# One down-projection chunk, loaded partly apart: 512 columns over seven transfer engines where it was 320 columns over four

## The chip, the cores and the metric

The kernel runs on one core of one Trainium2 chip. The metric is device time in microseconds (us) of one execution. The kernel before takes 265.25 us, the median of 3 runs (265.12 to 265.45).

## The reference, cut to what matters

One decode step of a block with attention and a gated MLP, 8 sequences, model width 1024, all in 32-bit floats:

```python
h  = x + attention(layernorm(x), wq, k_cache[-1024:], v_cache[-1024:], wo)
g  = layernorm(h) @ w_gate          # 1024 x 3584
u  = layernorm(h) @ w_up            # 1024 x 3584
h2 = h + (gelu(g) * u) @ w_down     # 3584 x 1024
```

Only the last product is touched by the change. Its 3584 rows are 28 chunks of 128 rows (q = 0 to 27); chunk 19 is the one that the change is about. There are only 8 rows of activations, so nearly all the work is to bring in the weights and caches.

## The kernel before, in words

**Stages.** The weights and caches pass once through one large buffer in on-chip memory (`space`, 2 x 16384 columns of 128 partitions), in the order wq, k, v, wo, gate and up (`gu`), down (`dn`), each with large transfers of 128 partitions, all issued by SyncE (SP) through the helper `move` (L89 to L92; its DMA start is on L91). A transfer is issued as soon as the part of the buffer that it overwrites has been used. Matmuls (4 copies of the 8 activation rows make 32 columns of weights for TensorE, PE) run when a transfer has landed; a wait for a transfer is a wait until all 16 transfer engines have finished their part of it.

**Transfers and engines.** A transfer's rows (one a partition) are dealt evenly over the transfer engines: 128 rows over all 16, 8 rows each; 4 rows over four engines, one row each, which the words of the change call the first four. Each engine works through its own queue in the order of issue, so an engine that got more bytes, or was held up, is late in all that follows.

**Down.** `PARTS = (8, 8, 4, 4, 2, 1)` (L27) cuts chunks 0 to 26 into six transfers, wd0 to wd5; here they are called the first to the sixth `dn` transfer. Chunk 27 comes in two transfers of its own (`ends`). The issue loop is L424 to L443, that of the ends L446 to L449. Chunk 19 is the last one of the third transfer (chunks 16 to 19). The last 320 columns (`SIDE_COLS`) of chunk 19 are not in that transfer, which so has 8 x 15104 B per engine in place of 8 x 16384 B; they come just ahead of it in 8 small transfers into `w_side` (L434 to L437): each has 4 partitions, 4 apart, hence the first four engines get one row of 5120 B (4 shares of 320 columns) from each of them, 40960 B in all. Row p of a small transfer's partitions holds 4 rows of the chunk, at different places ("shares").

**What the side rows need.** Chunk 19's activations stand transposed in `at` for the whole chunk. For `w_side` they must stand by partition as the shares do: four more transposes of shifted windows of `hm` (L396 to L399, windows of 48 columns from `SIDE_ROWS`) write them into PSUM behind the chunk transposes, ScalarE (ACT) copies them into `at_side` (L406). VectorE (DVE) copies the ordinary ones to `at` (L400).

**Down matmuls** (L457 to L474): in pairs of chunks, four matmuls of 512 columns a pair into four row groups of one bank `ya`. For chunk 19's second half there is one of 192 columns (L462) and four of 320 columns from `w_side` over 48 partitions (L472). Then `ya` is copied to `d1` by DVE (L476), chunk 26 goes to two other banks (L485), `d1` is added there by matmuls with `add2` (L485 too), chunk 27 follows (L497), ACT copies the two banks out (L500), and two transfers of 64 KB write the result.

Of the kernel before, what the change touches and what calls it, by code (L numbers as in the profile page):

```python
# [7 lines left out]
P = 128  # L8
B = 8
D = 1024  # L10
# [8 lines left out]
N = 512  # L19
# [6 lines left out]

PARTS = (8, 8, 4, 4, 2, 1)  # L27
SIDE = 19
SIDE_COLS = 320
SIDE_ROWS = (0, 16, 64, 80)  # L30
ENDS = (128, 128)
TAIL = 2

# [4 lines left out]
class Flow:  # L38
# [42 lines left out]
    def run(self, engine, make, *waits, mark=True):  # L81
        ins = self.start(engine, make, waits)
        if not mark:
            return None
        self.done[engine] += 1
        ins.then_inc(self.own[engine], 1)
        return self.own[engine], self.done[engine]
# [7 lines left out]
def decode_block(nc, x, wq, kt, v, wo, gu, dn, side, ends, outs):  # L95
# [8 lines left out]
    fl = Flow(nc)  # L104
    run, move = fl.run, fl.move
# [4 lines left out]
    def sb(name, *shape):  # L110
        return nc.alloc_sbuf_tensor(name, list(shape), F32).ap()
# [25 lines left out]
    ta, tb, ya = bank("ta", N), bank("tb", N), bank("ya", N)  # L137
# [10 lines left out]
    ident = sb("ident", P, P)  # L148
# [6 lines left out]
    qz = [sb(f"qz{hf}", P, 2, 10 * 32) for hf in range(2)]  # L155

    h_sb = sb("h_sb", P, D)

    w_side = sb("w_side", 64, len(SIDE_ROWS), SIDE_COLS)
    zero = [run("gpsimd", lambda e, t=t: e.memset(t, 0.0)) for t in (*qz, h_sb, w_side)]  # L160

    spread = sb("spread", P, CP, B)
    run("gpsimd", lambda e: e.tensor_copy(
# [14 lines left out]
    own = sb("own", P, HB)  # L178
# [4 lines left out]
    def transposes(pt, src, n, ready, clear, rows=P):  # L183

        t = pt[:, 0:n * rows].rearrange("p (n r) -> p n r", n=n)
        tok = None
        for i in range(n):
            tok = run("tensor", lambda e, i=i: e.transpose(  # L188
                t[:, i, :], src[:, i * P:(i + 1) * P], ident[:rows, :rows]),
                id_ok, ready, clear, mark=(i == n - 1))  # L190
        return t, tok
# [36 lines left out]
    for hf in range(2):  # L228
        w, w_in, wb = wq_t[hf]
        q_ps = (acc, tb)[hf]  # L230
        for c in range(NC):
            for j in range(NQ):
                tok = run("tensor", lambda e, c=c, j=j: e.matmul(  # L233
                    q_ps[32 * j:32 * j + 32, :], xt[c], w[:, c, j * N:(j + 1) * N],
                    start=(c == 0), stop=(c == NC - 1)),
                    w_in, x_ok, mark=(c == NC - 1 and j == NQ - 1))
        free[wb] = tok
        q_sb = sb(f"q{hf}", P, N)
        tok = run("vector", lambda e: e.tensor_scalar(q_sb, q_ps, scale, None, op0=ALU.mult), tok)
        acc_free = tok  # L240
        qt, tok = transposes(ta, q_sb, N // P, tok, ta_free)
# [54 lines left out]
    for hf in range(2):  # L296
        p_sb, p_ok, share, sh_ok = ps[hf]
        pt = sb(f"pt{hf}", P, KC, P)
        p0, tok0 = transposes(ta, p_sb[:, 0:W // 2], KC // 2, p_ok, ta_free)
# [5 lines left out]
        for c in range(KC):  # L305
            for r in range(NQ):
                s, half = divmod(r, 2)
                tok = run("tensor", lambda e: e.matmul(  # L308
                    o3[32 * r:32 * r + 32], pt[:, c, 32 * r:32 * r + 32],
                    v_t[:, s, c, half * HB:(half + 1) * HB, :],  # L310
                    start=(c == 0), stop=(c == KC - 1)),
                    v_in, ta_free, ya_free, mark=(c == KC - 1 and r == NQ - 1))
# [50 lines left out]
    for k, nb in enumerate(SETS):  # L363
        pair = big[1 - k].rearrange("p (s n) -> p s n", s=2)
        clear = (ps[1][1], h_ok)[k]
        for s in range(2):
            if k == 0:
                w, w_in, wb = load(gu[k][s], f"gu{k}_{s}", "c n", c=NC)
            else:
                n = NC * nb * N  # L370
                w = space[:, place:place + n].rearrange("p (c n) -> p c n", c=NC)
                w_in = move(f"gu{k}_{s}", w, gu[k][s], (used[0, 0], half_used)[s])
                place += n
            for c in range(NC):
                for j in range(nb):
                    tok = run("tensor", lambda e: e.matmul(  # L376
                        pair[32 * j:32 * j + 32, s, :], ht[c], w[:, c, j * N:(j + 1) * N],
                        start=(c == 0), stop=(c == NC - 1)),
                        w_in, ht_ok, clear, mark=(c in (NC // 2 - 1, NC - 1) and j == nb - 1))
                if (k, s, c) == (0, 1, NC // 2 - 1):  # L380
                    half_used = tok
            used[k, s] = tok
            if s == 0:
                rows = 32 * nb
                ge = sb(f"ge{k}", P, N)
                g_ok = run("scalar", lambda e: e.activation(
                    ge[:rows], pair[:rows, 0, :], AF.Gelu_apprx_tanh), tok)
        hm = sb(f"hm{k}", P, N)
        tok = run("vector", lambda e: e.tensor_mul(hm[:rows], ge[:rows], pair[:rows, 1, :]), tok, g_ok)  # L389
        hp, tok = transposes(ta, hm[:rows], N // P, tok, ta_free, rows)  # L390
        if k == 1:

            g, i = divmod(SIDE - q0, N // P)
            sp = ta[0:48, N - 32 * len(SIDE_ROWS):N].rearrange("p (s m) -> p s m", m=32)
            assert g == 0 and rows * (N // P) + 32 * len(SIDE_ROWS) <= N
            for s, c0 in enumerate(SIDE_ROWS):  # L396
                tok = run("tensor", lambda e: e.transpose(
                    sp[:, s, :], hm[0:32, i * P + c0:i * P + c0 + 48], ident[0:32, 0:32]),
                    mark=(s == len(SIDE_ROWS) - 1))  # L399
        ta_free = run("vector", lambda e: e.tensor_copy(  # L400
            at[:, q0:q0 + nb * (N // P), :].rearrange("p (j i) m -> p i j m", j=nb),
            hp.rearrange("p i (j m) -> p i j m", j=nb)), tok)
        at_ok.append(ta_free)
        if k == 1:
            at_side = sb("at_side", 48, len(SIDE_ROWS), 32)
            side_ok = run("scalar", lambda e: e.copy(at_side, sp), ta_free)  # L406
        q0 += nb * (N // P)

# [10 lines left out]
    def rows_of(q):  # L419
        return ring[:, slot(q)]  # L420
# [3 lines left out]
    for i, n in enumerate(PARTS):  # L424


        a, b = slot(q0), slot(q0) + n
        clear = used[0, 1] if a >= base else used[1, 0] if b * D <= place // 2 else used[1, 1]
        assert b <= SLOTS and (a >= base or b <= base)
        if q0 <= SIDE < q0 + n:  # L430
            assert SIDE == q0 + n - 1

            side_in = fl.sem("w_side")
            for h, src in enumerate(side):  # L434
                p0 = h % 4 + 32 * (h // 4)
                fl.start("sync", lambda e: e.dma_start(w_side[p0:p0 + 13:4], src), [zero[-1]]).then_inc(
                    side_in, 16)  # L437
            side_in = side_in, 16 * len(side)
            here = move(f"wd{i}", space[:, a * D:b * D - SIDE_COLS], dn[i], clear)
        else:  # L440
            here = move(f"wd{i}", ring[:, a:b], dn[i], clear)
        arrived.update((q, here) for q in range(q0, q0 + n))
        q0 += n  # L443
    blocks = []
    c0 = 0
# [11 lines left out]
    for q in range(0, first, 2):  # L457
        for i in range(NQ):
            e2, ch = divmod(i, 2)
            r = ch if q in SLOW else i  # L460
            n = N - SIDE_COLS if (q + e2, ch) == (SIDE, 1) else N
            tok = run("tensor", lambda e: e.matmul(  # L462
                ya[32 * r:32 * r + 32, 0:n], at[:, q + e2, :],
                rows_of(q + e2)[:, ch * N:ch * N + n],
                start=(r not in opened), stop=(q == first - 2)),
                arrived[q + e2], at_ok[(q + e2) * P >= SETS[0] * N],
                mark=(q == first - 2 and i == NQ - 1))
            opened.add(r)
            if n < N:
                for s in range(len(SIDE_ROWS)):  # L470
                    r = 1 + 2 * (s % 2)
                    run("tensor", lambda e: e.matmul(  # L472
                        ya[32 * r:32 * r + 32, n:N], at_side[:, s, :], w_side[0:48, s, :],
                        start=False, stop=False), side_in, side_ok, mark=False)  # L474
    d1 = sb("d1", P, N)
    d1_ok = run("vector", lambda e: e.tensor_copy(d1, ya), tok)  # L476

# [125 lines left out]
```

## Time and profile before

| what | value |
|---|---|
| median of 3 runs | 265.25 us |
| span of the profiled execution, first to last instruction | 263.8 us |
| read from memory, and rate over the span | 111.18 MB, 422 GB/s |
| PE busy | 137.9 us (52%) |
| DVE, ACT, POOL busy | 23.3, 10.9, 5.5 us |

The profiled execution has no time of its own beside its span; the median of the runs is 1.45 us above the span. In the rows below, a line of the chain of waits is "start, length, what"; a line of a window table is "window, length, busy time of an engine and number of instructions, granted TensorE clock, share of the 16 transfer engines that was busy, GB/s". Packets are counted in the window in which they start, with their whole length, so a share of a short window can be over 1. A packet of under 512 B stands at the end of an engine's part of each transfer: it is the engine's report that its part is done. So the number of such packets in a window is the number of engines that have finished a transfer in it.

### The profile page before, as it was taken

How to read it: one execution, taken by the hardware profiler on the slowest of the kernel's cores; microseconds unless marked ns; L12 is line 12 of the kernel's file. 1: busy time of each engine (PE TensorE's matmuls, PEld its weight loads, DVE VectorE, ACT ScalarE, POOL GpSimd, SP SyncE). 2: the span in 40 equal slices, each digit the busy share in tenths (PEclk: the TensorE clock that was granted, in tenths of full speed). 3: DMA queues.
4: the chain of work that ended last, by engine and by line, in shares of the span. 5: the costliest groups of instructions: out<-in, count | busy, mean ns of one | idle time of the engine just before them, and what ended most of it. 6: DMA issues, size and time to landing. Idle time of an engine off the chain costs nothing.

```text
span 263.8 us, 2071 instructions
## 1 busy us (share of the span) xinstructions
PE 137.9 (52%) x958; PEld 40.2 (15%) x958; DVE 23.3 (9%) x55; ACT 10.9 (4%) x17; POOL 5.5 (2%) x15
## 2 busy tenths in 40 slices
PE   0015806804905906806707707718509676589875
PEld 0011201201201301301202202112102111123122
DVE  0320100100010020200200100160000200010001
ACT  1110000000010020110000000020000000000000
POOL 8000000000000000000000000000000000000000
PEclk9999975985985895975975956986965979599999
DMA  8998998999799989999998999999899989999995
GB/s 318 482 437 358 477 477 378 420 467 477 328 467 477 420 388 457 470 388 437 447 477 348 460 457 437 398 437 477 360 422 455 477 365 465 412 422 452 390 415 203
DMA packets 3256, 111.44 MB, mean 422 GB/s; under 512 B 392, under 2 KB 648, under 8 KB 1072
## 3 DMA queue, kind: packets, MB, share of 16 engines
q1 hardware_dynamic: 3088, 111.22, 98.0%
q8 instruction: 7, 0.11, 0.2%
q10 hardware_dynamic: 160, 0.10, 0.1%
q14 instruction: 1, 0.01, 0.0%
HBM read 111.18 MB, written 0.13 MB: 422 GB/s over the span
## 4 chain that ended last, share of the span: by engine, by line
DMA 78%; PE 20%; SPq 0%; issue 0%; ACT 0%
DMA w<-gu 20%; DMA w<-wq 16%; DMA w<-kt 12%; DMA w<-wo 11%; DMA w<-v 11%; DMA w<-dn 9%; PE big L376 6%; PE big L261 4%; PE tb L233 4%; PE tb L308 3%; PE ya L336 3%; SPq L91 0%; PE acc L485 0%; ACT o_fin L500 0%; PE tb L485 0%
## 5 line engine op out<-in xcount | busy, mean ns | idle before, releaser
L376 PE MATMUL big<-w,ln_t 128*32 128x512 f32 x224 | 36.1, 730 | 21.6 <-DMA w<-gu 21.6
L261 PE MATMUL big<-w,qz 128*32 128x512 f32 x128 | 18.8, 753 | 20.2 <-DMA w<-kt 20.2
L336 PE MATMUL ya<-w,ot 128*32 128x512 f32 x128 | 18.1, 729 | 19.6 <-DMA w<-wo 19.6
L462 PE MATMUL ya<-w,at 128*32 128x512 f32 (+1 forms) x104 | 16.4, 590 | 3.6 <-DMA w<-dn 3.6
L376 PEld LDWEIGHTS big<-w,ln_t 128*32 128x32 f32 x224 | 9.0, 130 | 47.3 <-issue 25.8
L308 PE MATMUL tb<-w,pt 128*32 128x512 f32 x64 | 9.1, 732 | 9.8 <-DMA w<-v 9.8
L233 PE MATMUL tb<-w,ln_t 128*32 128x512 f32 x64 | 9.2, 743 | 9.2 <-DMA w<-wq 9.2
L308 PE MATMUL acc<-w,pt 128*32 128x512 f32 x64 | 8.5, 694 | 8.6 <-DMA w<-v 8.6
L233 PE MATMUL acc<-w,ln_t 128*32 128x512 f32 x64 | 8.6, 699 | 7.5 <-DMA w<-wq 7.5
L188 PE MATMUL ta<-ident,ln_xn 64*128 64x64 f32 x16 | 2.1, 304 | 19.3 <-DVE ln_xn L214 19.3
L261 PEld LDWEIGHTS big<-w,qz 128*32 128x32 f32 x128 | 4.8, 135 | 33.6 <-issue 23.4
L336 PEld LDWEIGHTS ya<-w,ot 128*32 128x32 f32 x128 | 5.0, 132 | 31.2 <-issue 31.2
L462 PEld LDWEIGHTS ya<-w,at 128*32 128x32 f32 x104 | 4.2, 109 | 15.4 <-issue 10.3
L389 DVE TENSOR_TENSOR hm<-ge,big 128x512 f32<-128x512 f32 (+1 forms) x2 | 1.4, 686 | 56.7 <-PE big L376 56.7
L270 DVE TENSOR_REDUCE nmax<-big 128x1 f32<-128x1024 f32 x2 | 2.5, 1225 | 35.7 <-PE big L261 35.7
L272 ACT ACTIVATE p<-big,nmax 128x1024 f32<-128x1024 f32 x2 | 2.2, 1114 | 78.1 <-DVE nmax L270 78.1
L308 PEld LDWEIGHTS tb<-w,pt 128*32 128x32 f32 x64 | 2.5, 131 | 15.7 <-issue 15.7
L188 PEld LDWEIGHTS ta<-ident,ln_xn 64*128 64x128 f32 x16 | 1.7, 200 | 20.1 <-DVE ln_xn L214 20.1
L233 PEld LDWEIGHTS tb<-w,ln_t 128*32 128x32 f32 x64 | 2.3, 134 | 15.5 <-DMA w<-wq 9.4
L308 PEld LDWEIGHTS acc<-w,pt 128*32 128x32 f32 x64 | 2.4, 126 | 14.1 <-issue 14.1
L233 PEld LDWEIGHTS acc<-w,ln_t 128*32 128x32 f32 x64 | 2.4, 126 | 13.0 <-issue 13.0
L205 ACT ACTIVATE ln_sd<-ln_ve 64x1 f32<-64x1 f32 x2 | 0.4, 203 | 69.3 <-DVE ln_ve L204 69.3
(81 smaller groups left out, 53.3 us busy)
## 6 DMA issues: line engine op xcount, KB each, us to landing
w<-gu SPq DMA_DIRECT2D x2, 6144.0 KB, 23.7
w<-dn SPq DMA_DIRECT2D x2, 4096.0 KB, 27.1
w<-dn SPq DMA_DIRECT2D x1, 2048.0 KB, 20.0
w<-dn SPq DMA_DIRECT2D x1, 1888.0 KB, 24.1
w<-dn SPq DMA_DIRECT2D x1, 1024.0 KB, 22.1
w<-dn SPq DMA_DIRECT2D x1, 512.0 KB, 22.9
w<-ends SPq DMA_DIRECT2D x2, 256.0 KB, 23.1
w_side<-side SPq DMA_DIRECT2D x8, 20.0 KB
```

What stands on the lines that cost most here:

```text
L188: tok = run("tensor", lambda e, i=i: e.transpose(t[:, i, :], src[:, i * P:(i + 1) * P], ident[:rows, :rows]), id_ok, ready, clear, mark=(i ...
L205: tok = run("scalar", lambda e: e.activation(sd, ve, AF.Sqrt), tok)
L233: tok = run("tensor", lambda e, c=c, j=j: e.matmul(q_ps[32 * j:32 * j + 32, :], xt[c], w[:, c, j * N:(j + 1) * N], start=(c == 0), stop=(c ...
L261: tok = run("tensor", lambda e: e.matmul(s_ps[32 * r:32 * r + 32, k0:k0 + N], qz[hf][:, s, c0:c0 + 32], k_t[:, s, half * HB + b, k0:k0 + N ...
L270: tok = run("vector", lambda e: e.tensor_reduce(out=nmax, in_=s_ps, axis=AX.X, op=ALU.max, negate=True), tok)
L272: p_ok = run("scalar", lambda e: e.activation(p_sb, s_ps, AF.Exp, bias=nmax, accum_out=tot), tok)
L308: tok = run("tensor", lambda e: e.matmul(o3[32 * r:32 * r + 32], pt[:, c, 32 * r:32 * r + 32], v_t[:, s, c, half * HB:(half + 1) * HB, :], ...
L336: tok = run("tensor", lambda e: e.matmul(ya[32 * r:32 * r + 32, :], ot[:, 2 * hf * REP + h + e2].rearrange("p r b -> p (r b)"), w[:, h + e ...
L376: tok = run("tensor", lambda e: e.matmul(pair[32 * j:32 * j + 32, s, :], ht[c], w[:, c, j * N:(j + 1) * N], start=(c == 0), stop=(c == NC ...
L389: tok = run("vector", lambda e: e.tensor_mul(hm[:rows], ge[:rows], pair[:rows, 1, :]), tok, g_ok)
L462: tok = run("tensor", lambda e: e.matmul(ya[32 * r:32 * r + 32, 0:n], at[:, q + e2, :], rows_of(q + e2)[:, ch * N:ch * N + n], start=(r no ...
```

## The change

Chunk 19's second half (512 columns) is now wholly loaded apart. `w_side` has 3 shares of 512 columns. Eight small transfers have 7 partitions (4 apart) with two shares each, 4096 B a row, for the first seven engines; four more have 4 partitions with the third share, 2048 B a row, for the first four. The third `dn` transfer has 14336 B a row in place of 15104 B. Since the shares are now runs of 28 rows, the activations are first laid into `hm_side` by two copies on ACT (zero elsewhere, by a fill on POOL), and three transposes of 64 columns take the place of four of 48; in the down matmuls three of 512 columns over 64 partitions take the place of one of 192 and four of 320.

```diff
-SIDE_COLS = 320
-SIDE_ROWS = (0, 16, 64, 80)
+SIDE_COLS = 512
+LOW = 7
+RUN = 4 * LOW
+SHARES = 3
+REST = P - 4 * RUN
...
-    w_side = sb("w_side", 64, len(SIDE_ROWS), SIDE_COLS)
-    zero = [run("gpsimd", lambda e, t=t: e.memset(t, 0.0)) for t in (*qz, h_sb, w_side)]
+    w_side = sb("w_side", 64, SHARES, SIDE_COLS)
+    hm_side = sb("hm_side", 32, SHARES, 64)
+    zero = [run("gpsimd", lambda e, t=t: e.memset(t, 0.0)) for t in (*qz, h_sb, hm_side, w_side)]
...
-            for s, c0 in enumerate(SIDE_ROWS):
+            part = hm[0:32, i * P:(i + 1) * P]
+            run("scalar", lambda e: e.copy(
+                hm_side[:, 0:2, :].rearrange("p s (h n) -> p (s h) n", h=2)[:, :, 0:RUN],
+                part[:, 0:4 * RUN].rearrange("p (g n) -> p g n", n=RUN)), hm_ok, zero[-1])
+            hs_ok = run("scalar", lambda e: e.copy(hm_side[:, 2, 0:REST], part[:, 4 * RUN:P]))
+            for s in range(SHARES):
                 tok = run("tensor", lambda e: e.transpose(
-                    sp[:, s, :], hm[0:32, i * P + c0:i * P + c0 + 48], ident[0:32, 0:32]),
-                    mark=(s == len(SIDE_ROWS) - 1))
+                    sp[:, s, :], hm_side[:, s, :], ident[0:32, 0:32]),
+                    hs_ok, mark=(s == SHARES - 1))
...
-                fl.start("sync", lambda e: e.dma_start(w_side[p0:p0 + 13:4], src), [zero[-1]]).then_inc(
-                    side_in, 16)
+                dst = w_side[p0:p0 + 4 * LOW - 3:4, 0:2] if h < 8 else w_side[h - 8:h - 8 + REST - 3:4, 2]
+                fl.start("sync", lambda e: e.dma_start(dst, src), [zero[-1]]).then_inc(side_in, 16)
...
-            n = N - SIDE_COLS if (q + e2, ch) == (SIDE, 1) else N
+            if (q + e2, ch) == (SIDE, 1):
+                for s in range(SHARES):
+                    r = 1 + 2 * (s % 2)
+                    run("tensor", lambda e: e.matmul(
+                        ya[32 * r:32 * r + 32, :], at_side[:, s, :], w_side[:, s, :],
+                        start=False, stop=False), side_in, side_ok, mark=False)
+                continue
...
-            if n < N:
-                for s in range(len(SIDE_ROWS)):
-                    r = 1 + 2 * (s % 2)
-                    run("tensor", lambda e: e.matmul(
-                        ya[32 * r:32 * r + 32, n:N], at_side[:, s, :], w_side[0:48, s, :],
-                        start=False, stop=False), side_in, side_ok, mark=False)
```

More of the change, by code (lines that the diff above doesn't have):

```diff
@@ L389, in decode_block @@
         tok = run("vector", lambda e: e.tensor_mul(hm[:rows], ge[:rows], pair[:rows, 1, :]), tok, g_ok)
+        hm_ok = tok
         hp, tok = transposes(ta, hm[:rows], N // P, tok, ta_free, rows)
@@ L393, in decode_block @@
             g, i = divmod(SIDE - q0, N // P)
-            sp = ta[0:48, N - 32 * len(SIDE_ROWS):N].rearrange("p (s m) -> p s m", m=32)
-            assert g == 0 and rows * (N // P) + 32 * len(SIDE_ROWS) <= N
-            for s, c0 in enumerate(SIDE_ROWS):
+            sp = ta[0:64, N - 32 * SHARES:N].rearrange("p (s m) -> p s m", m=32)
+            assert g == 0 and rows * (N // P) + 32 * SHARES <= N
+            part = hm[0:32, i * P:(i + 1) * P]
[4 more added lines that the diff above has]
+            for s in range(SHARES):
                 tok = run("tensor", lambda e: e.transpose(
-                    sp[:, s, :], hm[0:32, i * P + c0:i * P + c0 + 48], ident[0:32, 0:32]),
-                    mark=(s == len(SIDE_ROWS) - 1))
+                    sp[:, s, :], hm_side[:, s, :], ident[0:32, 0:32]),
+                    hs_ok, mark=(s == SHARES - 1))
         ta_free = run("vector", lambda e: e.tensor_copy(
@@ L404, in decode_block @@
         if k == 1:
-            at_side = sb("at_side", 48, len(SIDE_ROWS), 32)
+            at_side = sb("at_side", 64, SHARES, 32)
             side_ok = run("scalar", lambda e: e.copy(at_side, sp), ta_free)
@@ L460, in decode_block @@
             r = ch if q in SLOW else i
-            n = N - SIDE_COLS if (q + e2, ch) == (SIDE, 1) else N
+            if (q + e2, ch) == (SIDE, 1):
+                assert SIDE_COLS == N and q != first - 2 and {1, 3} <= opened
+                for s in range(SHARES):
[4 more added lines that the diff above has]
+                continue
             tok = run("tensor", lambda e: e.matmul(
-                ya[32 * r:32 * r + 32, 0:n], at[:, q + e2, :],
-                rows_of(q + e2)[:, ch * N:ch * N + n],
+                ya[32 * r:32 * r + 32, :], at[:, q + e2, :],
+                rows_of(q + e2)[:, ch * N:(ch + 1) * N],
                 start=(r not in opened), stop=(q == first - 2)),
@@ L551 @@
         for a, n, m in zip(at, PARTS, width)])
-    side = np.stack([
-        rows[SIDE, c0:c0 + 64, D - SIDE_COLS:] if c0 + 64 <= P else
-        np.concatenate([rows[SIDE, c0:, D - SIDE_COLS:], rows[SIDE, :c0 + 64 - P, D - SIDE_COLS:]])
-        for c0 in SIDE_ROWS], 1).reshape(2, 8, 4, len(SIDE_ROWS), SIDE_COLS)[:, 0:4]
-    side = side.transpose(0, 2, 1, 3, 4).reshape(8, 4, len(SIDE_ROWS), SIDE_COLS)
+    rest = rows[SIDE][:, D - SIDE_COLS:]
+    runs = rest[0:4 * RUN].reshape(2, 2, LOW, 4, SIDE_COLS).transpose(1, 3, 2, 0, 4)
+    side = np.concatenate([
+        runs.reshape(-1), rest[4 * RUN:].reshape(REST // 4, 4, SIDE_COLS).transpose(1, 0, 2).reshape(-1)])
     cuts = [sum(ENDS[:i]) for i in range(len(ENDS) + 1)]
@@ L564 @@
         "x": own(A_x).reshape(B, D), "wq": own(wq), "kt": own(kt), "v": own(v), "wo": own(wo),
-        "gu": np.concatenate(gus), "dn": dn, "side": own(side), "ends": ends,
+        "gu": np.concatenate(gus), "dn": dn, "side": side, "ends": ends,
     }
@@ L585 @@
         f0 += P * m
-    aps["side"] = [aps["side"][i] for i in range(8)]
+    flat, f0 = aps["side"], 0
+    aps["side"] = []
+    for rs, shares in [(LOW, 2)] * 8 + [(REST // 4, 1)] * 4:
+        m = rs * shares * SIDE_COLS
+        t = flat[f0:f0 + m]
+        aps["side"].append(t.rearrange("(p s n) -> p s n", p=rs, s=2) if shares == 2 else
+                           t.rearrange("(p n) -> p n", p=rs))
+        f0 += m
     flat, f0 = aps["gu"], 0
```

## The prediction

> **What bounds the kernel now.** I read the page first, then the chain of waits at the end, then the transfer packets in short windows.
>
> ```profile
> span 263.8 us, 2071 instructions
> q1 hardware_dynamic: 3088, 111.22, 98.0%
> q8 instruction: 7, 0.11, 0.2%
> HBM read 111.18 MB, written 0.13 MB: 422 GB/s over the span
> DMA 78%; PE 20%; SPq 0%; issue 0%; ACT 0%
> ```
>
> The queue with the weights keeps the 16 transfer engines busy for 98% of the span. So bytes are the bound: 422 GB/s over 16 engines at 98% is 422 / 16 / 0.98 = 26.9 KB per us for one busy engine (an estimate from these rows). The third row is the other thing to keep: 7 packets of 16 KB that fetch instructions.
>
> ```profile
> 237.10 22.92 DMA w<-dn
> 260.06 0.43 PE acc L485 x8
> 260.48 0.22 PE tb L485 x8
> 260.70 0.39 PE acc L485 x8
> 261.09 0.22 PE tb L485 x8
> 261.31 0.26 PE acc L497 x8
> 261.60 0.48 ACT o_fin L500 x2
> ```
>
> The end hangs on the sixth `dn` transfer (landed at 260.02), followed by a fixed run of matmuls, copies and the output. A transfer counts as landed when its slowest engine is done, so the question is which engines are late, and by how much. The next rows count engines that report a transfer finished (the packets under 512 B): the first `dn` transfer, before the side loads, in 234.7 to 235.4 and 236.1 to 236.8; the third, behind them, in 248.9 to 249.6 and 250.3 to 251.0; the fifth's early ones in 256.4 to 257.2.
>
> ```profile
> DMA packets 23, 0.43 MB, mean 609 GB/s; under 512 B 10, under 2 KB 10, under 8 KB 10
> DMA packets 19, 0.43 MB, mean 609 GB/s; under 512 B 6, under 2 KB 6, under 8 KB 6
> DMA packets 24, 0.28 MB, mean 399 GB/s; under 512 B 6, under 2 KB 6, under 8 KB 6
> DMA packets 32, 0.36 MB, mean 509 GB/s; under 512 B 10, under 2 KB 10, under 8 KB 10
> DMA packets 53, 0.31 MB, mean 389 GB/s; under 512 B 5, under 2 KB 5, under 8 KB 25
> ```
>
> Ten engines are early and six are some 1.3 us late before the side loads. Behind them six are early and ten late: the four side engines were early ones and have joined the late. At the end five are early. What makes an engine late is an instruction fetch; the rows are those of 255.0 to 256.5, then two stretches near the end:
>
> ```profile
> q1 hardware_dynamic: 76, 0.57, 93.2%
> q8 instruction: 1, 0.02, 4.5%
> ...
> 259.45:260.35 0.90, 0.00 (x0) 1.00 0.73 282
> 257.00:257.70 0.70, 0.00 (x0) 1.00 1.00 415
> ```
>
> One fetch takes 4.5% of 16 engines x 1.5 us = 1.08 us of one engine. Seven fetches on the page, and 16 - 4 - 5 = 7 engines late without a side load: one fetch each, on seven different engines. At 257 all engines are busy; from 259.45 on only 0.73 of the engines work (11 of 16 is 0.69; records overlap a little): five idle while eleven finish. These five are what the change can use.
>
> **The change part by part.**
>
> *Bytes per engine, in the third `dn` transfer and the side loads ahead of it.* The big transfer loses 8 x (15104 - 14336) = 6144 B on every engine. The first four engines carry 8 x 4096 + 4 x 2048 = 40960 B of side rows, as before (8 x 5120); engines five to seven get 8 x 4096 = 32768 B that they didn't have. At 26.9 KB per us:
> - engines that carry no side rows, the fetched ones among them: -6144 B, -0.23 us;
> - the first four: -0.23 us, plus four more packets and reports. The 2-KB stretch above gives 282 / 0.73 / 16 = 24.1 KB per us, or 85 ns a packet against 76 at the full rate, so 9 ns a packet: four packets and as many reports are some 0.05 to 0.07 us. Net -0.17 us;
> - engines five to seven: 32768 B = 1.22 us, plus eight packets with reports 0.1, less 0.23: +1.1 us. If they are early ones they have 1.3 us to spare and stay ahead of the rest by about 0.1 to 0.2 us.
>
> So the slowest engine moves by -0.17 to -0.23 us, if engines five to seven are unfetched. I take -0.2 us.
>
> *Landing to end.* The last stretch must follow:
>
> ```profile
> 246.88 3.64 PE L462 MATMUL ya<-w,at 128*32 128x512 f32 x32 [1.20 <-DMA w<-dn]
> ...
> 254.19 1.27 PE L472 MATMUL ya<-w_side,at_side 48*32 48x320 f32 x8
> ...
> 256.31 1.92 PE L462 MATMUL ya<-w,at 128*32 128x512 f32 x16 [0.86 <-DMA w<-dn]
> ...
> 258.79 1.06 PE L462 MATMUL ya<-w,at 128*32 128x512 f32 x8 [0.55 <-DMA w<-dn]
> ...
> 260.06 0.43 PE L485 MATMUL acc<-w,at 128*32 128x128 f32 x8 [0.20 <-DMA w<-dn]
> ```
>
> At each of the last four stages PE waited for the transfer (0.86, 0.55, 0.20 us idle in the last three), so each stage starts 0.2 us earlier when its transfer lands 0.2 us earlier; DVE's copy of `ya` follows the fifth transfer and moves with it. The output and what lies around the span are unchanged.
>
> *Matmuls of the side rows.* Before: 1280 columns in 1.27 us plus one matmul of 192; after: 1536 columns, at the same rate 1.52 us, and none of 192. That is at most +0.25 us in the stage that ends before 256.31. Its cover is the 0.86 us of idle time there (0.66 when the transfer behind lands 0.2 us earlier). It is nothing; without that cover it would be up to +0.25.
>
> *Transposes and the two ACT copies ahead of them.*
>
> ```profile
> 237.54 0.29 PE L397 MATMUL ta<-ident,hm 32*48 32x32 f32 x4
> 237.87 0.56 DVE L400 COPY at<-ta 128x384 f32<-128x384 f32 x1 [0.87 <-PE ta L397]
> 238.46 0.26 ACT L406 COPY at_side<-ta 48x128 f32<-48x128 f32 x1 [16.12 <-DVE at L400]
> ```
>
> A copy on ACT takes 0.26 us for 48x128; two smaller ones, 0.5 us in all at most, now stand between `hm` and the side transposes, beside the 0.55 us of the chunk transposes. The side transposes (three, about 0.2 us) wait for ACT; behind them in PE's queue wait the residual matmuls (L453) and all down matmuls, and DVE's copy to `at`. Bounds: 0 and +0.5 us; I take +0.3. PE then works through chunks 0 to 7 and afterwards sits idle 1.20 us, for the second `dn` transfer, so the delay is hidden. `at` and `at_side` are wanted some 13 us later.
>
> *Issue.*
>
> ```profile
> 222.11 5.08 SPq L436 DMA_DIRECT2D w_side<-side  x8
> 227.24 10.29 SPq L91 DMA_DIRECT2D w<-dn  x4
> ```
>
> Twelve issues in place of eight, 5.08 / 8 = 0.64 us each, put the third `dn` transfer's issue (227.24) off by 2.5 us, to some 229.8. An engine reaches it only after finishing the second one, which landed just before the 246.88 above, on the early engines some 1.3 us sooner: from about 245 on. Cover: 15 us. The sixth is issued at 237.10 as before, after a wait for PE. The fills on POOL (one more, one longer) lie at the start, where POOL's only work is:
>
> ```profile
> POOL 8000000000000000000000000000000000000000
> ```
>
> The Trainium skill, "DMA: Bandwidth & Descriptors", section "Rules for kernel authors", says that transfers under 64 KB are mostly overhead; section "Anatomy of one DMA" has about 2 us fixed for each (on GpSimd's path). By that, four more of them would cost up to 8 us, an estimate. Here the eight side loads and 40960 B moved four engines by the same 1.3 to 1.6 us that the bytes alone take, so the trace does not bear it out for engines whose queues are full.
>
> **Sum** for the profiled execution: 263.8 - 0.2 = 263.6; the median is 1.45 above that span, so 265.25 - 0.2 = **265.05 us**.
>
> **The rivals.**
>
> *One of engines five to seven is a fetched one.* Then it has its 1.08 to 1.3 us and the side rows: 1.1 us later than the slowest now, and every transfer behind waits for it: 265.25 + 1.1 = 266.3 us, slower. It decides as soon as one of the three is fetched; the other engines' gain doesn't count then. No view names engines. But an engine's packets follow each other without a gap, so I stepped back from the fetches packet by packet. Rows (windows of some ns; 410 is a 4-KB packet in 10 ns, 1638 a 16-KB one, the others are 64-KB packets in 10, 5 and 6 ns):
>
> ```profile
> 7.35:7.36 0.01, 0.00 (x0) 1.00 0.99 410
> 7.50:7.51 0.01, 0.00 (x0) 1.00 15.11 6554
> 46.17:46.19 0.01, 0.00 (x0) 0.50 6.35 1638
> 7.33:7.33 0.01, 0.00 (x0) 1.00 30.25 13107
> 87.09:87.10 0.01, 0.00 (x0) 0.50 6.71 1638
> 7.58:7.59 0.01, 0.00 (x0) 1.00 25.21 10923
> 111.53:111.53 0.01, 0.00 (x0) 1.00 6.68 1638
> ```
>
> The first fetch (46.18) stands 16 packets behind 7.51, where the engine had just moved a 4-KB packet of `x`: (46.18 - 7.51) / 16 = 2.417 us each. The second (87.09) stands 33 packets behind 7.33, also 2.417 each, on an engine without any packet of `x`; the third (111.53) is 43 behind 7.58, 2.417 again, on such an engine too. `x` has 8 rows, one for each of eight engines. So the first fetch is on one of the eight engines with `x` but on none of the four with side rows, which leaves engines five to eight; the next two are on the upper eight. Fetches that go from engine to engine in order would start on the eighth and then take the ninth, tenth and so on; starting on the fifth to seventh, the second would still be among the `x` engines. That is the evidence against this rival; the order of the other four I couldn't follow. 14%.
>
> *The fetches move.* The program of PE gets a little shorter, so its last fetch comes a little later, or the engines shift by one. A later fetch holds the same engine for the same 1.08 us while it still has work: no change. A shift by one engine downwards is the rival above, and is in its chance.
>
> *A load of seven rows isn't dealt over seven engines.* If one engine took all 7 rows, it would have 56 x 4096 B in place of 8 x 4096: +7.3 us, 272 us, slower. Four and eight rows are dealt one to an engine in this trace; seven isn't shown. 3%. The Trainium skill, same page, section "Why a DMA increments its semaphore by 16 and not by 1", says that the number of engines is the largest up to 16 that divides the rows, which makes it seven; no run here has shown that.
>
> *The time of the end isn't the engines' alone.* If DVE's copy and the `d1` matmuls set the end with an earlier cause, or the small packets cost more than 9 ns, the 0.2 us is lost: 265.2 to 265.5. 10%. For it speaks that PE's last idle time is only 0.20 us; against it, that the chain ahead of it starts at a transfer as well.
>
> **How the numbers follow.** Forecast 265.05 (70%, 264.8 to 265.3 with the scatter of the runs, 0.33 us), lost gain 10%, a fetched engine 14%, one engine for all 3%; 3% for a gain over 0.5 us that I can't name. I count 0.2% (0.53 us) as what a measurement can tell from no change. A gain of 0.2 us is 0.08%, so forecast and lost gain are both "within"; faster 0.04, within 0.78, slower 0.18. The range takes in forecast and lost gain, 264.8 to 265.6; beyond it lie the 17% of the two slow cases and the unnamed gain.
>
> **What would show it.** In the profile after: third-transfer reports with nearly all engines in one group, five to seven close ahead of the rest, and in the last us before the last landing 14 of 16 engines busy in place of 11; the sixth `dn` transfer landing at about 259.8; PE's idle times at the four stages as now. Wrong would be: one engine's report 1 us behind all others, an eighth fetch, the side matmuls without an idle gap behind them, or a landing at 259.8 with an end that doesn't follow.

## The result, and the profile after

The changed kernel takes 266.80 us, the median of 5 runs (266.68 to 267.15), beside 265.23 us for the kernel before (5 runs, 265.12 to 265.45): 1.0063 times as long, with a 95% interval of 1.0051 to 1.0075. Two more series of the same code (below) gave 1.0042 and 1.0039. So it is slower by 1.0 to 1.6 us, where no change that can be measured was the likeliest. The profiled execution took 267.07 us.

From the page of the kernel after, the lines that answer to the first five of the prediction:

```profile
span 265.7 us, 2069 instructions
q1 hardware_dynamic: 3168, 111.22, 97.5%
q8 instruction: 7, 0.11, 0.2%
HBM read 111.18 MB, written 0.13 MB: 419 GB/s over the span
DMA 71%; PE 24%; SPq 3%; issue 1%; DVE 0%; ACT 0%
```

The bytes are the same, and there are still seven instruction fetches. The span grew by 1.9 us. The chain has moved: PE has 24% of it where it had 20%.

The engines' reports of the third `dn` transfer in the kernel after, by windows 249.0 to 249.8, 250.3 to 251.3 and 252.0 to 252.5; the packets under 512 B are the reports:

```profile
DMA packets 26, 0.33 MB, mean 407 GB/s; under 512 B 4, under 2 KB 4, under 8 KB 4
DMA packets 39, 0.44 MB, mean 442 GB/s; under 512 B 11, under 2 KB 11, under 8 KB 11
DMA packets 17, 0.26 MB, mean 524 GB/s; under 512 B 1, under 2 KB 1, under 8 KB 1
```

Before, six engines were early, ten late, and none behind those. Now four are early, eleven late, and one is more than 1 us behind the last of the late ones. The transfer has landed only when this one is done. Near the end there are two such engines. The row of the window table for the kernel after, 261.30 to 262.00 (busy time there is POOL's, which is idle; the share of the transfer engines is the sixth figure):

```profile
261.30:262.00 0.70, 0.00 (x0) 1.00 0.13 50
```

0.13 of 16 engines is two: fourteen have no more work while two still move their last packets.

The chain of the kernel after, its end; columns are start, length, what:

```profile
230.99 21.72 DMA w<-dn
252.72 0.14 issue
252.85 4.25 PE ya L479 x14
257.11 1.99 PE ya L475 x6
259.10 2.76 PE ya L479 x24
...
261.88 0.69 DVE d L487
...
263.56 0.48 ACT o_fin L511 x2
```

Before, the chain hung on the sixth `dn` transfer with PE waiting in front of it. Here it hangs on the third, which landed at 252.71, and from there PE works without a pause to the end. Why PE has become the bound is in the clock column (before the share of the transfer engines) of the window table of PE, kernel after:

```profile
252.50:254.00 1.50, 1.15 (x7) 0.99 0.95 404
254.00:257.40 3.40, 3.40 (x12) 0.50 0.99 407
257.40:262.00 4.60, 4.60 (x46) 1.00 0.68 272
```

For 3.4 us PE was granted half its clock, just after it had waited 2.01 us for the late transfer. So there are two things to explain: one engine behind all others, and, in this execution, a PE that could not catch up.

### The profile page after: what moved, and what is told of

It is laid out like the page before. It is cut to its first block, busy times and chain, and to the rows that moved or that the text cites. A ratio compares the mean times of both kernels' runs of the same rounds, so it can differ in the third digit from the quotient of the medians.

```text
span 265.7 us, 2069 instructions
## 1 busy us (share of the span) xinstructions
PE 140.4 (53%) x953; PEld 40.7 (15%) x953; DVE 23.3 (9%) x55; ACT 11.3 (4%) x19; POOL 6.0 (2%) x16
## 4 chain that ended last, share of the span: by engine, by line
DMA 71%; PE 24%; SPq 3%; issue 1%; DVE 0%; ACT 0%
DMA w<-gu 21%; DMA w<-v 11%; DMA w<-kt 11%; DMA w<-wo 11%; DMA w<-wq 8%; DMA w<-dn 8%; PE big L380 6%; PE acc L237 4%; PE acc L312 4%; PE ya L340 3%; PE big L265 3%; SPq L447 3%; PE ya L479 3%; PE ya L475 1%; DVE d L487 0%
## 5 line engine op out<-in xcount | busy, mean ns | idle before, releaser
L265 PE MATMUL big<-w,qz 128*32 128x512 f32 x128 | 17.8, 716 | 21.3 <-DMA w<-kt 21.3
L479 PE MATMUL ya<-w,at 128*32 128x512 f32 x102 | 17.7, 633 | 2.1 <-DMA w<-dn 2.0
L312 PE MATMUL acc<-w,pt 128*32 128x512 f32 x64 | 9.6, 771 | 9.3 <-DMA w<-v 9.3
L237 PE MATMUL acc<-w,ln_t 128*32 128x512 f32 x64 | 9.8, 779 | 7.6 <-DMA w<-wq 7.6
L312 PE MATMUL tb<-w,pt 128*32 128x512 f32 x64 | 8.5, 691 | 8.7 <-DMA w<-v 8.7
```

The lines of the kernel that those rows point to most:

```text
L237: tok = run("tensor", lambda e, c=c, j=j: e.matmul(q_ps[32 * j:32 * j + 32, :], xt[c], w[:, c, j * N:(j + 1) * N], start=(c == 0), stop=(c ...
L265: tok = run("tensor", lambda e: e.matmul(s_ps[32 * r:32 * r + 32, k0:k0 + N], qz[hf][:, s, c0:c0 + 32], k_t[:, s, half * HB + b, k0:k0 + N ...
L312: tok = run("tensor", lambda e: e.matmul(o3[32 * r:32 * r + 32], pt[:, c, 32 * r:32 * r + 32], v_t[:, s, c, half * HB:(half + 1) * HB, :], ...
L479: tok = run("tensor", lambda e: e.matmul(ya[32 * r:32 * r + 32, :], at[:, q + e2, :], rows_of(q + e2)[:, ch * N:(ch + 1) * N], start=(r no ...
```

## The experiments

The theory, A: one of engines five to seven takes a side load and an instruction fetch; it then has both delays, some 1.1 us each, and everything waits for it. The rivals, B: something else that the change does costs the time (the four more loads and their later issue, the copies on ACT, the side matmuls). C: the load itself makes the engines later than its bytes, or engines six and seven are always the slow ones. A speaks of a certain number of engines with both; B doesn't care how many rows a load has; C would be the same in every execution.

**rows4, rows5, rows6**: the changed kernel, with fewer rows in the eight loads of seven rows and all else in place; the rows left out are missing from the product. The edit (5 and 6 in place of 4 for the others):

```diff
-                dst = w_side[p0:p0 + 4 * LOW - 3:4, 0:2] if h < 8 else w_side[h - 8:h - 8 + REST - 3:4, 2]
+                dst = w_side[p0:p0 + 4 * 4 - 3:4, 0:2] if h < 8 else w_side[h - 8:h - 8 + REST - 3:4, 2]
+                src = src[0:4] if h < 8 else src
```

> The kernel after, but its eight seven-row side loads bring only their first four rows, so engines five to seven carry no side rows (48 rows of chunk 19's second half are left out of the product). Everything else, matmuls, ACT copies and twelve issues, is as in the kernel after. Theory 1 (an engine with both an instruction fetch and side rows sets the end): no engine has both, so the third dn transfer lands in one late group, none 1 us behind, and the time falls below the kernel before by the 0.2 us of the forecast: 265.0, at most 265.3. Theory 2 (PE sets the end, by the side matmuls of 512 columns and the clock that it is granted): PE's work is unchanged, so 266.7 stays.

> The same with five rows: the fifth engine carries side rows too (32 rows of the chunk left out). Theory 1: 265.0 if the fifth engine is not a fetched one, about 266.2 if it is; in the profile one engine reports the third dn transfer, or a later one, 1 us behind all others only in the second case. Theory 2: 266.7.

> The same with six rows (16 rows of the chunk left out). Theory 1: the kernel after had two such late engines at the end, so at least one of the fifth and sixth must be fetched: about 266.2, one engine 1 us behind. Theory 2: 266.7.

**again**: the changed kernel a second time.

> The kernel after once more, on the same chip as the three others. Both theories 266.7. What it tells: whether the half clock that PE was granted at 254.0 to 257.4 in the first profile is there again. Theory 1 alone wants some 266.3 and leaves 0.4 us open; theory 2 wants the same dip in this profile, and the end behind PE's matmuls rather than behind a landing.

Measured, beside 265.28 us for the kernel before (29 runs, 265.11 to 265.65):

| kernel | us, median (lowest to highest, runs) | ratio, 95% interval |
|---|---|---|
| rows4 | 265.05 (264.85 to 265.38, 11) | 0.9989, 0.9981 to 0.9998 |
| rows5 | 265.02 (264.94 to 265.28, 11) | 0.9993, 0.9984 to 1.0001 |
| rows6 | 266.00 (264.82 to 266.54, 12) | 1.0016, 1.0001 to 1.0030 |
| again | 266.23 (266.09 to 266.83, 5) | 1.0042, 1.0030 to 1.0054 |

B falls: rows4 and rows5 have all twelve loads, the copies and the side matmuls, and cost nothing. The step comes with the sixth and seventh row. And rows6 is not the one time of 266.2 that was expected: five runs lie at 264.82 to 265.11 and seven at 265.94 to 266.54, with nothing between. C, as a fixed delay, doesn't give two groups. The same code on the same chip takes the step in one execution and not in the next. The repeated kernel came out at 266.23 us, below the 266.7 expected: two of its five runs lie at 266.76 and 266.83, three at 266.09 to 266.23.

The reports show it engine by engine. rows5, the third `dn` transfer, windows 248.7 to 249.5 and 250.2 to 251.0:

```profile
DMA packets 29, 0.35 MB, mean 443 GB/s; under 512 B 5, under 2 KB 5, under 8 KB 5
DMA packets 30, 0.31 MB, mean 387 GB/s; under 512 B 11, under 2 KB 11, under 8 KB 11
```

rows6, in an execution of 264.99 us, windows 248.7 to 249.5 and 249.9 to 251.0:

```profile
DMA packets 26, 0.33 MB, mean 407 GB/s; under 512 B 4, under 2 KB 4, under 8 KB 4
DMA packets 42, 0.48 MB, mean 432 GB/s; under 512 B 12, under 2 KB 12, under 8 KB 12
```

The repeated kernel (266.83 us), windows 248.7 to 249.5, 250.1 to 251.0 and 251.7 to 252.2:

```profile
DMA packets 25, 0.30 MB, mean 374 GB/s; under 512 B 5, under 2 KB 5, under 8 KB 5
DMA packets 36, 0.43 MB, mean 473 GB/s; under 512 B 9, under 2 KB 9, under 8 KB 9
DMA packets 16, 0.23 MB, mean 459 GB/s; under 512 B 2, under 2 KB 2, under 8 KB 2
```

Count one delay for a fetch and one for a side load. Up to the third transfer six of the seven fetches have happened, and a load of n rows holds n engines. Then late engines + 2 x engines behind must be n + 6. It is so in rows5 (11 = 5 + 6), in rows6 (12 = 6 + 6) and in the repeated kernel (9 + 2 x 2 = 7 + 6), as in the first profile after (11 + 2 x 1 = 7 + 6). The two delays simply add up on an engine that has both.

In the first profile after, the engine behind can also be followed by itself. Ten engines end the second `dn` transfer by 245.47, six at 246.51 to 246.68: as many as there were fetches until then. Of the 56 packets of 4 KB of the side loads, 48 start between 244.94 and 246.31, which is eight for each of six loaded engines. The other eight follow each other from 246.65 to 247.94, each with its report, on an engine that was among the late six. The window from 246.9 to 247.9 holds six of them (the packets between 2 and 8 KB) and six reports; all else is of the third transfer:

```profile
DMA packets 42, 0.45 MB, mean 455 GB/s; under 512 B 6, under 2 KB 6, under 8 KB 12
```

No 2-KB packet comes behind them, as it would on the first four engines: a 14336-B packet starts at 247.945, then seven more, and the report is the one at 252.21. So the engine behind was late by a fetch, has side rows too, and is one of engines five to seven.

**pad6 and pad7**: is it the load alone? The kernel before, its transposes and matmuls untouched, with two or three rows of zeros added to each of its eight side loads (7 in place of 6 for pad7):

```diff
-                fl.start("sync", lambda e: e.dma_start(w_side[p0:p0 + 13:4], src), [zero[-1]]).then_inc(
+                fl.start("sync", lambda e: e.dma_start(w_side[p0:p0 + 4 * 6 - 3:4], src), [zero[-1]]).then_inc(
...
+    side = np.concatenate([side, np.zeros((8, 6 - 4) + side.shape[2:], side.dtype)], axis=1)
```

> The kernel before with its matmuls, transposes and copies untouched; only its eight side loads have six rows in place of four, the added two rows being zeros that fall on the fifth and sixth engines (8 x 5120 B each). Theory 1, as the last runs left it (the sixth engine takes an instruction fetch in some executions and not in others): two groups of times, about 265.3 and 266.2 to 266.5, like the six-row kernel. Rival (the new transposes, ACT copies and 512-column matmuls are what makes the slow runs slow): one group at 265.3.

> The same with seven rows, 8 x 5120 B of zeros on each of engines five to seven. Theory 1: slow in nearly every execution, 266.3 or more, one or two engines 1 us behind the rest. Rival: 265.3. On the half clock: if it follows from the late landing, PE is granted half in the last 12 us here too and some runs stand at 266.8 or above; if it follows from the longer side matmuls, PE stays at full clock and the runs stand at 266.1 to 266.5.

Beside 265.34 us before (17 runs, 265.09 to 265.78), pad6 took 266.56 us: four runs at 265.06 to 265.60 and eight at 266.46 to 266.86 (1.0032, interval 1.0016 to 1.0047). pad7 took 266.67 us, all six runs at 266.52 or more (266.52 to 267.83; 1.0056, interval 1.0043 to 1.0069). So six or seven rows in the loads are enough to bring the loss, two groups included. The profiled execution of pad6 (266.47 us), windows 248.9 to 249.6, 250.3 to 251.2 and 252.0 to 252.5:

```profile
DMA packets 23, 0.28 MB, mean 398 GB/s; under 512 B 5, under 2 KB 5, under 8 KB 5
DMA packets 33, 0.37 MB, mean 413 GB/s; under 512 B 10, under 2 KB 10, under 8 KB 10
DMA packets 15, 0.23 MB, mean 459 GB/s; under 512 B 1, under 2 KB 1, under 8 KB 1
```

10 + 2 x 1 = 6 + 6 again. The chain of pad6, its end:

```profile
237.62 23.73 DMA w<-dn
261.34 0.04 issue
261.39 0.43 PE acc L485 x8
...
262.97 0.48 ACT o_fin L500 x2
```

Here the chain looks like that of the kernel before; the sixth `dn` transfer lands at 261.34 in place of 260.02, and the end follows. This is the plain price of the engine behind, 1.3 us, without any loss on PE. pad7's profile (267.83 us) has both, with the matmuls of the kernel before; the window table of PE:

```profile
254.00:258.00 4.00, 1.88 (x12) 1.00 0.99 411
258.00:261.50 3.50, 3.35 (x16) 0.51 0.77 304
```

So the half clock isn't due to the longer side matmuls. PE idles for over 2 us of the four before 258.00, since the engine behind appears there with the fourth transfer, and has half a clock afterwards.

**steps and marks**: can the engines be told apart in one trace? steps adds fifteen small loads of 1 to 15 rows of 1 KB to the kernel before, marks four of 5, 6, 7 and 8 rows of 4 KB; each ran twice.

```diff
+    for i, k in enumerate((5, 6, 7, 8)):
+        fl.start("sync", lambda e: e.dma_start(
+            arena[16 * i:16 * i + k, i, :], wq[1][16 * i:16 * i + k, i, 0:W]), []).then_inc(marks_in, 16)
```

> The kernel before with fifteen more small loads between the second wq load and the first kt load, of 1, 2, ... 15 rows of 1024 B, into memory that isn't used yet: the first engine gets 15 packets more, the second 14, and so on to none for the sixteenth. So from 43 us on the engines stand in order of their number, some 0.05 us apart, and each instruction fetch can be put on its engine. Theory 1: the seven engines are all from the sixth to the sixteenth. Open: whether they are neighbours that start at the eighth (my prediction), or another set. The time itself, some 0.8 us above the kernel before, tells nothing.

> The same kernel a second time. If each fetch has its engine for good, the same seven in the same order as in the first run; if the set moves from execution to execution, as the two groups of the six-row kernel say, another order or another set.

> The kernel before with four more loads between the second wq load and the first kt load, of 5, 6, 7 and 8 rows of 4096 B, into memory that isn't used yet. The first five engines get four 4-KB packets each there, the sixth three, the seventh two, the eighth one, the others none; so an instruction fetch can be followed back, packet by packet, to the kind of engine that it is on. Theory 1 as it stands (the fetched seven are drawn from the sixth engine on, another draw in each execution): no fetch on an engine with four marks; the sixth to eighth each in some executions. My prediction's picture (always the eighth and its six upper neighbours): a fetch on the engine with one mark, none on those with two or three. Time about 266, which tells nothing.

> The same kernel in another execution. Under theory 1 the fetches with one, two and three marks are others, or come at other times, than in the first; if each fetch has its own engine, they are the same.

steps took 268.40 and 268.44 us (before 265.34; some 0.8 us more was expected, it was 3.1), and its small packets left gaps between each other, so an engine could not be followed through them: inconclusive. marks took 266.35 and 266.39 us (before 265.19). In its first execution most fetches fit several engines. In its second the first five fetches fit best to engines with neither a mark nor a packet of `x`; the sixth fits best to an engine with three marks, which would be the sixth engine, though other packets fit at two places. That alone decides nothing, but it isn't the order that I had read from the kernel before, where the first fetch was on an engine with `x`.

**groups and third.** The changed kernel's times spread over 1.2 us (265.94 to 267.15 in the 15 runs of its three series), those of the kernel before over 0.3 to 0.7 us in a series. Is that PE, which falls behind in some executions? groups spreads the matmuls of chunks 16 and 17 over four row groups in place of two, as those of chunks 18 and 19 are already, so that PE has less to do late; third is the changed kernel a third time.

```diff
-SLOW = (*range(0, 8), 16, 17)
+SLOW = (*range(0, 8),)
```

> The kernel after, with chunks 16 and 17 also spread over four row groups (SLOW holds chunks 0 to 7 alone), so that PE needs some 0.9 us less for the stage behind the third dn transfer. On the 0.4 to 0.7 us that some slow runs take beyond the late landing: if they are PE's, held up at half clock behind the late third transfer so that it is still at the fifth one's matmuls when the last transfers land, then PE now keeps up, and the runs fall together at 266.1 to 266.3. If they have another cause (a later landing still, the output), both levels stay, 266.1 to 266.2 and 266.7 to 267.1. The late engine itself is untouched in both, so nothing falls to 265.3 unless a draw of engines spares the sixth and seventh.

> The kernel after a third time, beside the one above on the same chip. Both levels again (266.1 to 266.2 and 266.7 to 267.1); if the seven fetched engines are neighbours in a ring of the sixth to sixteenth with any start, 3 starts in 11 spare the sixth and seventh, and some run should be as fast as 265.1; ten slow runs so far had none.

Beside 265.26 us before (10 runs, 265.12 to 265.46), groups took 266.53 us (six runs, 265.96 to 267.14; 1.0049, interval 1.0035 to 1.0063), and third 266.37 us (five, 265.94 to 266.71; 1.0039, interval 1.0027 to 1.0051). The timeline of groups shows that PE kept up, with an idle time, in the brackets, ahead of each of the last transfers:

```profile
257.06 1.92 PE L479 MATMUL ya<-w,at 128*32 128x512 f32 x16 [1.05 <-DMA w<-dn]
259.92 1.06 PE L479 MATMUL ya<-w,at 128*32 128x512 f32 x8 [0.94 <-DMA w<-dn]
261.16 0.43 PE L496 MATMUL acc<-w,at 128*32 128x128 f32 x8 [0.17 <-DMA w<-dn]
```

It spreads no less (neither one level nor the two that were expected), so PE isn't the whole of the spread; what else is, I could not settle. PE's share can be read from single profiles. The end of the chain of third, which had its full clock in this stretch:

```profile
237.47 23.97 DMA w<-dn
261.44 0.04 issue
...
263.04 0.48 ACT o_fin L511 x2
```

Its last copies begin at 263.04, where the kernel before has 261.60: +1.44 us, by the engine behind. In the first profile of the same code they begin at 263.56, with PE at half clock: 0.52 us more.

groups also gave the clearest trace of fetches. Rows of its window table, as in the prediction, in pairs: the packet at which the engine can be told, and the fetch (1638 or 2048 is that of a 16-KB packet in 10 or 8 ns):

```profile
7.45:7.45 0.01, 0.00 (x0) 1.00 25.22 10923
46.15:46.16 0.01, 0.00 (x0) 1.00 8.42 2048
7.66:7.67 0.01, 0.00 (x0) 1.00 18.92 8192
87.49:87.50 0.01, 0.00 (x0) 1.00 8.29 2048
7.17:7.18 0.01, 0.00 (x0) 1.00 1.42 585
219.62:219.63 0.01, 0.00 (x0) 1.00 6.36 1638
```

The first fetch lies 16 packets of 2.419 us behind a 64-KB packet at 7.451, on an engine without a packet of `x`; so does the second, 33 packets behind 7.665. The sixth leads back to the 4-KB packet of `x` at 7.175. In the execution of the kernel before, the first fetch was on an `x` engine and the second and third were not. The two executions differ in where the fetches fall, against where the rows fall. (The traces show the fetches against the loads, not the engines' own numbers, so it is not shown which of the two moves.)

## Why the prediction was wrong

- *Bytes bound the kernel; a fetch holds one engine for about 1.08 us; seven fetches, seven engines.* Right. Late + 2 x behind = rows + 6 in every profile that was counted (rows4, third and groups too: 10 = 4 + 6, 13 = 7 + 6 and 11 + 2 x 1 = 7 + 6), and the seventh fetch can still come: pad7 has 3 early and 13 late engines (13 = 7 + 6) and none behind at the third transfer, one behind at the fourth.
- *Bytes per engine, -0.2 us on the slowest if none of the loaded engines is fetched.* Right, as far as it was conditional: rows4 and rows5, which fulfil the condition, came out 0.23 and 0.26 us below the kernel before (the interval of rows5 just takes in no change).
- *Matmuls of the side rows, +0.25 us hidden by 0.86 us of idle time.* Hidden, but mis-sized. rows5, its timeline:

```profile
251.36 2.77 PE L480 MATMUL ya<-w,at 128*32 128x512 f32 x14 [0.82 <-DMA w<-dn]
254.06 1.90 PE L476 MATMUL ya<-w_side,at_side 64*32 64x512 f32 x6
256.21 1.92 PE L480 MATMUL ya<-w,at 128*32 128x512 f32 x16 [0.25 <-DMA w<-dn]
258.65 1.06 PE L480 MATMUL ya<-w,at 128*32 128x512 f32 x8 [0.52 <-DMA w<-dn]
259.92 0.43 PE L497 MATMUL acc<-w,at 128*32 128x128 f32 x8 [0.20 <-DMA w<-dn]
```

  Six instructions take 1.90 us, not 1.52, and leave 0.25 us of the cover: the matmuls cost 0.63 us more than the 1.27 before, not at most 0.25. The prediction added up the columns of all of them. But in the trace two into different row groups start together: before, the eight instructions start in four pairs, some 0.28 us apart; in rows5 the six start as two pairs and two alone, some 0.43 us apart, since the first and the third share (L476, r = 1) go to the same row group. So both have four steps, of 320 and of 512 columns; 1.27 x 512 / 320 = 2.03 us would have been the nearer estimate. The stages behind are as foreseen: 0.52 and 0.20 us of idle time, as before (0.55, 0.20), and a sixth transfer landed at 259.88 in place of 260.02.
- *Transposes and the two copies on ACT, some +0.3 us hidden.* Hidden: rows4 and rows5 have them all.
- *Issue, 0.64 us each, third transfer put off to 229.8, hidden.* It was issued at 230.99 (the chain above), 0.7 us for most of the side loads. Hidden all the same: rows4 and rows5 issue as late and lose nothing. The 3% of the chain that is now given to SP is time beside full transfer queues.
- *A load of seven rows on seven engines.* The sums above, with n = 5, 6 and 7, hold only if each row takes an engine of its own. The Trainium skill, "DMA: Bandwidth & Descriptors", section "Why a DMA increments its semaphore by 16 and not by 1", which the prediction could cite only without a run, agrees with these counts.
- **The failed step is the dismissal of the rival "one of engines five to seven is a fetched one".** Its price was right: 266.3 us, and the three series of this kernel lie at 265.94 to 267.15. Its chance, 14%, was wrong. The prediction followed three fetches of one execution, found the first on one of engines five to eight and the next two on the upper eight, and concluded that they "start on the eighth and then take the ninth, tenth and so on". Silently it took what one execution showed for a property of the kernel; that the fetches move was weighed too, but only as an effect of the change. The runs show that it differs from execution to execution, like a draw. Read from the times, with six rows the sixth engine was hit in 15 of 24 executions (7 of 12 in rows6, 8 of 12 in pad6), with seven rows the sixth or the seventh in 27 of 27 (the changed kernel 15, pad7 6, groups 6). With five rows it was none of 11, with four none of 11 in rows4; the kernel before, with four, has never shown the step. The first five engines are spared, in all that ran here; the sixth and seventh are not.
- *What would show it wrong.* "One engine's report 1 us behind all others" is what came, already in the first profile.
- *Not foreseen:* PE's half clock after the late landing, some 0.5 us in one profile of the changed kernel beside another. It was seen in three profiles with an engine behind (after, its first repetition and pad7), and not in three others that have one (third, pad6 and groups, of which groups has less work for PE late). The wait alone doesn't decide: pad6 waited 2.37 us, longer than the 2.01 of after. In all 14 profiles the granted clock changes only on a grid of 3.41 us (after: to half at 226.68 and again eight such steps later, at 253.99), and it goes with how busy PE was in the grid stretch before. These stretches, ahead of the late matmuls, in pad7, after, pad6 and third:

```profile
254.67:258.09 3.42, 1.21 (x9) 1.00 0.99 409
250.57:253.98 3.41, 1.40 (x11) 1.00 0.96 407
249.01:252.43 3.42, 1.48 (x16) 1.00 1.02 434
255.44:258.85 3.41, 1.85 (x14) 1.00 0.98 398
```

  Half the clock followed the first two, the full clock the others; pad6's wait lay across a grid edge. Counted over all 14 profiles, half followed all 150 full-clock stretches with PE busy below 0.41 of the time, full all 373 with 0.47 or more, and of the 20 between, 8 had half. So where the late landing falls on the grid counts too; this is read from traces, no run varied it. In steps_again the half clock came late as well (255.86), and cost nothing that shows.

The cause of the changed kernel's loss is therefore shown: the load of rows six and seven brings it, alone and without the rest of the change, and it comes and goes with the engine behind. Open stays how a fetch's engine is chosen. The profiles whose fetches could be followed fit seven neighbours in a ring made of the sixth to the sixteenth engine, with a start that changes. With eleven equal starts the sixth engine would be hit in 7 of 11 executions, 15 of 24, as it was; but engines six and seven would both be spared in 3 of 11, and in none of 27 they were. So a ring with equal starts doesn't fit, and the ring itself is argued, not shown. Open too is the rest of the spread among executions with an engine behind, and how many of the runs without a profile had half the clock late.

A version of the change with five rows beats the kernel before by nothing that can be told: rows5's 0.26 us leaves out 32 rows, and with their bytes back on the engines less would be left. No version that computes the whole and is faster was found.

## What to carry to other kernels

Where the end hangs on the slowest of 16 transfer engines, count the engines' reports per transfer: they show early, late and behind engines, and delays that add up. But a free engine in one profile is one draw; ask for its place in several executions before work is put on it, and put it only on engines that were free in all of them. A dismissal that rests on one execution deserves the chance of the draw, not that of a proof.

## What the runs showed of the hardware that was not expected

- Which engine takes an instruction fetch, against the rows of a load, differs between executions of one program: two groups of times in rows6, 1.1 us apart by their medians (264.99 and 266.10), 0.83 by their nearest runs.
- The Trainium skill, "Runtime: NRT & Kernel Launch", section "Instruction fetch mechanics", says that instructions come in 16-KiB blocks over a queue of their own, and that crossing a block is mostly hidden. The seven packets and 0.11 MB of the instruction queue agree with the size. In this kernel, bound by bytes, they are not hidden: each delays one transfer engine by about 1.1 us, and a fetch and a side load on one engine cost it its 0.4 to 0.6%.
- PE was granted half its clock for about 3.4 us after a wait of 2.01 us, when it worked again without a pause (0.50 in the row of 254.00 to 257.40), but not after one of 2.37 us (pad6). It went by PE's busy share in the 3.41-us stretch before: 0.41 in after, 0.43 in pad6, in the narrow band in which both were seen. In two profiles of one kernel the end came 1.44 us late without it (third) and 1.96 us late with it.
